# One mask tile, a gate ring of two, one scaled product on another engine and a refitted order in a fused attention and expert kernel

## The chip, the cores and the metric

The kernel runs on one core of one Trainium2 chip. The metric is the device time of one execution in microseconds; the median of three runs of the kernel before is 354.05 us (353.97 to 354.15). PE is TensorE (matrix products), ACT is ScalarE, DVE is VectorE, POOL is GpSimd and SP is SyncE. POOL and SP do little work of their own here; both mainly issue DMA transfers, each in its own fixed order.

## The reference

Four batches of eight heads, 768 tokens and 64 numbers a head go through attention with a sliding window of 128 and four sink tokens that every query sees. The result, 3072 tokens of 512 numbers, goes through four experts, each a layer 512 to 1024 with a ReLU and a layer 1024 to 512. Every expert sees every token, and its output is scaled by the token's share for it.

```python
keep = is_sink | in_window                    # 4 sinks, window of 128
scores = np.where(keep, q @ k.T / sqrt(D), -1e9)
a = softmax(scores); attn = a @ v             # per batch and head
x = attn.transpose(0, 2, 1, 3).reshape(B * S, H * D)
p = domain_probs / domain_probs.sum(-1, keepdims=True)
out = sum(p[:, e:e+1] * (np.maximum(x @ w1[e], 0) @ w2[e]) for e in range(4))
```

## The kernel before

**Work.** Each batch b has three groups g of 256 tokens. Attention of a group and a pair of heads is a scores step (L708, 64-row matmuls, `sps`), an exponential on ACT (L733, `aT`), a product with a 0/1 mask on DVE (L727, L742), a values step (L767, L774, `od`), a normalization (L801 to L819, `onat`) and a transposition into `xT`, by PE (L838) or by a DMA transpose (L791). A `sinks` step (L669) needs the transposed keys and queries `qkT` of all six token blocks of its batch. An expert's work on one group is a unit (b, g, e). The first two groups of batch 0 (the early groups) run plainly: the first layer at L1118, the second at L1579, with the outputs scaled on DVE as they are summed over the experts (L1589 for expert 0, L1591 for the others). All other groups use a form with seven products in place of eight (P1 to P7) in both layers. Their first layer either has tokens in the columns ("gated", L1208, with DVE multiplying by the token's share from a `gates` tile, L1241) or is "turned" (L1320, with the share as a scale per row on ACT or DVE, L1338, L1341, L1345, and a DMA transpose of the result). There are 20 units of each kind. The second layer of both is L1493, and the sums of its operands are formed at L1434.

**Loads.** POOL issues the loads of weights (L331, L341), of q and k (`qkn`, L251) and of v (L318). SP issues the DMA transposes of `qkn` to `qkT` (L263), the loads of `gates` (L478), the DMA transposes of turned units and the stores of `out`. A batch's transposes overwrite the `qkT` of the batch before and so wait for its last scores. Loads of `qkn` reuse buffers that the transposes free. After the last transpose of a batch, POOL makes a tiny copy (`held`, L1703), so that the next batch's loads start behind it.

**Gates.** A `gates` tile holds the shares of one unit's 256 tokens, repeated over 128 partitions, 128 KB. There are `NGATE` of them, used in turn; the load for a unit waits until the unit that used the tile before it has finished.

**Masks.** Three tiles are used: `low` (the mask in a form that PE can add to the scores, for batch 0's first group), `mask0` for group 0 and `mask1` for groups 1 and 2. The order of the blocks in `GROUPS` fixes which columns of a scores tile are which block.

**Order.** All engines run an order that is written out when the kernel is built. A planner in the kernel keeps a clock per engine (`t["pe"]`, `t["act"]`, ...), with lengths that are constants in the code, and appends PE's next step by priorities (`DUE`, `LEAD`, `SHARE_OF`, `LOW_PRODUCT`, ...). Work of ACT and DVE goes into a list with the time at which it can start and how long it may wait, and is taken out by that due time:

```python
def later(engine, ready, slack, run):
    pend.append((ready, ready + slack, engine, run))
```

So a different constant moves steps on every engine, and each engine's own waits do the rest on the chip.

Of the kernel before, what the change touches and what calls it, by code (L numbers as in the profile page):

```python
# [16 lines left out]
def kernel(  # L17
# [12 lines left out]
    nc = tc.nc  # L30
# [33 lines left out]
    EXPERTS = {(1, 0): (0, 2, 1, 3), (1, 1): (3, 2, 1, 0), (1, 2): (3, 2, 1, 0), (2, 2): (2, 0, 3, 1), (3, 1): (3, 2, 1, 0)}  # L64
# [7 lines left out]
    LOW_SECOND = 2.7  # L72
    HIGH_PRODUCT = 1.9
    EARLY = -0.01
    MASK = 5000
    GATE = 800
    GATE0 = 300
    FORM = 6000
    TOKEN = 3000
    MARGIN = 500  # L80
    HOLD = 0
    FULL = 7
    STEP0 = 0.03
    READY = 40
    REST = 3000
    LANDS = 0
    SCALED = 300
    SHARED = 2
    MARGIN1, MARGIN2 = 4000, 14000
    OWNED_READ = 152  # L90
    WIDE = 2
    OPEN = 2.5
    SOON = 34000
    NEARLY = 2
# [5 lines left out]
    ONE = 2  # L100
    HOLDS = 2
    MORE = 2
    BOTH = 1
    PAIR = 0
    OVER = 4
    ALONE = 2.0
    BEHIND = 1500
    CHORES = 3
    BIASED = 1
# [89 lines left out]

    landed = {}  # L200
    ROW = {64: 12.8, 128: 22.6, 256: 41.7, 512: 79.8, 1024: 156.2}

    def lands(key, rows, cols, *deps):
        issued = pool(0, *deps, fixed=880)
        at = max(t["sw"], issued + 1500)
# [253 lines left out]

    gate_sb = {}  # L460
    gate_tiles = [consts.tile([P, 2, 2, P], FP32, name=f"gates{i}") for i in range(NGATE // 2)]

# [8 lines left out]
    def load_gate(pair, e):  # L471

        i = len(gate_sb) % NGATE
        x = gate_tiles[i // 2][:, i % 2]
        if FIRST <= len(gate_sb) < NGATE:
            nc.vector.memset(x[0:1, 0, 0:1], 0.0)
            dve(1, fixed=150)
        nc.sync.dma_start(  # L478
            out=x.rearrange("p t n -> p (t n)"), in_=gate_rows[pair, e].rearrange("t n -> (t n)").partition_broadcast(P),
        )  # L480
        gate_sb[pair, e] = x
        sp(takes=300)

# [26 lines left out]
    for tb in (2, 3):  # L510
# [18 lines left out]
    LOW = 32768.0  # L529
    low = [lent[:, 5 * P:8 * P], lent[:, 8 * P:12 * P]]  # L530
    nc.vector.tensor_scalar(
        out=low[0].rearrange("p (n q) -> p n q", n=3)[:, 0::2], in0=two, scalar1=LOW, scalar2=-LOW, op0=ALU.mult, op1=ALU.add,
    )
    nc.vector.tensor_scalar(out=low[0][:, P:2 * P], in0=own, scalar1=-LOW, scalar2=None, op0=ALU.mult)
    nc.vector.memset(low[0][0:NSINK, 0:2 * P], 0.0)
    nc.vector.reduce_sum(
        out=sel2, in_=ident.rearrange("p (n c) -> p n c", c=32)[:, :, 0:2 * NSINK].rearrange("p n (a j) -> p n a j", a=2), axis=AX.X,
    )
    x = low[1].rearrange("p (n c q) -> p n c q", n=2, c=2)
    nc.scalar.activation(out=x[:, :, 0], in_=two, func=AF.Copy, scale=-LOW)  # L540
    nc.scalar.activation(out=x[:, :, 1], in_=two, func=AF.Copy, scale=LOW, bias=-LOW)
    mask0 = consts.tile([P, 3 * P], BF16, name="mask0")
    mask1 = consts.tile([P, 4 * P], BF16, name="mask1")
    made = []

    def make_mask(i):
        def run(engine):
            x = (mask0, mask1)[i]
            if i:
                nc.scalar.activation(out=x, in_=low[i], func=AF.Copy, scale=1 / LOW, bias=1.0)  # L550
                act(4 * P)
            else:
                nc.vector.tensor_scalar(out=x, in0=low[i], scalar1=1 / LOW, scalar2=1.0, op0=ALU.mult, op1=ALU.add)
                dve(3 * P)
            made.append(i)
        later(("dve", "act")[i], (24000.0, 11700.0)[i], 8000, run)
# [132 lines left out]
    def scores(b, hp, g, more=False):  # L689
# [10 lines left out]
        if biased:  # L700
            for ph in range(2):
                nc.tensor.matmul(sps[ph][:, 0:w], lhsT=ident, rhs=low[min(g, 1)], start=True, stop=False, skip_group_check=True)
            pe(2 * w, ready, n=2)
# [18 lines left out]
        if b == 0:  # L722
            part = join(2, masked)
        else:
            def mask_both(at):
                def run(engine):
                    nc.vector.tensor_mul(a, a, m[:, None, :].to_broadcast([P, 2, w]))  # L727
                    masked(dve(2 * w, rate=1.92))
                later("dve", at, MASK, run)
            part = join(2, mask_both)  # L730
        for ph in range(2):
            def run(engine, ph=ph):
# [8 lines left out]
                def mask_one(engine):  # L741
                    nc.vector.tensor_mul(a[:, ph], a[:, ph], m)  # L742
                    part(dve(w, rate=1.92))
# [216 lines left out]
    class Mixture:  # L960


        def __init__(self):
# [13 lines left out]
            mine = [u for u in self.order if u[0] >= OWN]  # L977
            self.turning = set(mine[TURNED_UNITS[0]:len(mine) - TURNED_UNITS[1]])
            self.gated = [u for u in self.order if u not in self.turning]
            self.G, self.resting = {}, []  # L980
            self.T, self.T_at, self.fast, self.finished = {}, {}, {}, set()
# [43 lines left out]
        def opened(self, b, g, e):  # L1025
# [11 lines left out]
            def complete(at):  # L1037
                self.H_at[b, g, e] = at
                self.finished.add((b, g, e))
                if (b, g) >= PAIRS[0]:  # L1040
                    self.waiting.append((b, g, e))
                    load_gates()
                    if not TURNED_UNITS[1] and self.gated[-1] == (b, g, e):
                        self.rest_gates()
# [39 lines left out]
        def emit_first(self, what, ready):  # L1084
# [56 lines left out]
            def run(engine):  # L1141
# [5 lines left out]
                part(at)  # L1147
            later("dve", end, GATE0, run)

# [32 lines left out]
        def emit_fast(self, u, m, ready):  # L1182
# [40 lines left out]
            def gated(dst, src, half_, ready, slack, slot=None, then=None):  # L1223
# [16 lines left out]
                def run(engine):  # L1240
# [44 lines left out]
        def emit_turning(self, u, m, ready):  # L1285
# [47 lines left out]
            def gated(k, s, src, ready, slack, slot=None, then=None):  # L1333
                gate = own_gates[:, 2 * ((b - OWN) * NG + g) + s, e:e + 1]

                def run(engine):
                    if engine == "act":
                        nc.scalar.activation(out=src, in_=src, func=AF.Relu)  # L1338

                        def scaled(engine):  # L1340
                            nc.scalar.mul(X[k][:, :, s], src, gate)  # L1341
                            done(act(n))
# [3 lines left out]
                    done(dve(n, fixed=OWNED_READ))  # L1346

                def done(at):
                    if slot is not None:
                        take(slot, at)  # L1350
# [40 lines left out]
        def chore(self):  # L1391
# [40 lines left out]
            def form(engine):  # L1432
                x = steps.pop(0)
                x[0](*x[1:])  # L1434
                at = dve(QF * P, self.stored[-1] if (b, g) == PAIRS[0] else 0.0, rate=1.92)
                if steps:
                    go(form, self.until(b, g, e, "P6 P7".split()[len(steps) == 2]))
# [128 lines left out]
        def emit_second(self):  # L1566
# [20 lines left out]
            def run(engine):  # L1587
                if e == 0:
                    nc.vector.tensor_scalar(out=dst, in0=op, scalar1=sc, scalar2=None, op0=ALU.mult)  # L1589
                else:  # L1590
                    nc.vector.scalar_tensor_tensor(  # L1591
                        out=dst, in0=op, scalar=sc, in1=dst, op0=ALU.mult, op1=ALU.add,
                    )
# [5 lines left out]
            later("dve", end, 400, run)  # L1599
            self.since = 0  # L1600
# [36 lines left out]
    work = [sum(NFB * NDB * G * (1 if (b, g) < START[e] else 7 / 8) + NFB * NDB * G * (1 if (b, g) < PAIRS[0] else 7 / 8) for g in range(NG) for e in range(E)) for b in range(B)]  # L1637
    ahead, upto, loaded, wide, rowed = 0, 0.0, 0, 0, 0
    asked = []
# [22 lines left out]
    while mix.more() or att.more():  # L1662
# [28 lines left out]
        if x and t["pool"] < now + 1500 and free_ring(x):  # L1691
            loads.remove(x)
            x[0](*x[1:])
        if turns and (ahead < 2 or not mix.second) and landed.get(("qk", *turns[0]), 1e12) < now and (turns[0][0] <= ahead or turns[0][0] == ahead + 1 and not att.todo):
# [7 lines left out]
            if 0 < b < B - 1 and x[1] == NQB - 1:  # L1702
                nc.gpsimd.tensor_copy(out=held, in_=qkT[b][:, 1, NHP - 1, S - 2:S])  # L1703
                pool(2, turned_at[x])
                nat_loads(b + 1, range(NQB))
                turns += [(b + 1, tb) for tb in range(NQB)]
        flush(now)
        mix.tokens()
# [3 lines left out]
        if ahead + 1 < B and not att.more() and (ahead == 0 or (ahead + 1, 0) in turned_at) and (ahead == 0 or mix.done >= sum(work[:ahead]) * LEAD[ahead - 1]):  # L1712
            ahead += 1
            if ahead == 1:
                own_load()
            elif ahead == 2:
                own_made()
            att = Attention(ahead)
# [79 lines left out]
```

## Time and profile before

| | |
|---|---|
| median of three runs | 354.05 us |
| span of the profiled execution, first to last instruction | 351.9 us |
| outside the span (the median less the span) | 2.15 us |
| PE busy, share of the span | 346.2 us, 98% |
| DVE busy | 282.8 us, 80% |
| ACT busy | 208.3 us, 59% |
| POOL busy | 71.6 us, 20% |
| granted TensorE clock | 1.000 |
| moved by DMA | 45.61 MB, mean 130 GB/s |

A time of the profiled execution itself is not given beside its span; the median of the runs stands for it, and the 2.15 us between the two are taken as fixed. Busy time is the union of an engine's instructions. Matmuls overlap one another and their ends are modelled, so a busy PE can still have small pauses in it; they show only in the distances between the starts. In a row of the groups, the first part names the line, the engine, the operation and the tiles, then come the count, the busy time, the mean length of one in ns, and the idle time just before them with what ended it.

### The profile page before, as it was taken

To read this page: it belongs to the slowest core of one execution; us is meant where nothing else is said; L and a number is where in the kernel's file an instruction comes from. 1 tells how busy PE (TensorE), PEld (TensorE's weight loads), DVE (VectorE), ACT (ScalarE), POOL (GpSimd) and SP (SyncE) were. 2 spreads that over 40 slices of the span, in tenths; PEclk is the share of its full clock that TensorE was granted. 3 is DMA by queue.
4 is the path that set the end of the run, shared out by engine and by line. 5 is a ranking of instruction groups with operands and counts; after the bars stand their busy time and mean duration, and the time that the engine had idled before them with its cause. 6 is when DMAs were issued, how large, how long until landed. Compare 5 with 4: busy or idle time off the path is not lost.

```text
span 351.9 us, 9351 instructions
## 1 busy us (share of the span) xinstructions
PE 346.2 (98%) x3721; PEld 266.0 (76%) x3721; DVE 282.8 (80%) x672; ACT 208.3 (59%) x476; POOL 71.6 (20%) x89
## 2 busy tenths in 40 slices
PE   8999999999999999999999999999999999999996
PEld 3685769656789998998999886755856676666685
DVE  5886999878999999799898999578768586675740
ACT  6863624447874443647453539689589767666611
POOL 8946114330546206100152000000000000000000
PEclk9999999999999999999999999999999999999999
DMA  9999999999999999920999602545437733545441
GB/s 178 178 188 195 223 214 181 179 160 174 162 147 165 121 145 122 132 64 9 109 173 159 113 32 62 120 101 120 80 91 174 127 89 93 120 120 115 67 120 61
DMA packets 161032, 45.61 MB, mean 130 GB/s; under 512 B 144740, under 2 KB 156996, under 8 KB 160988
## 3 DMA queue, kind: packets, MB, share of 16 engines
q0 software_dynamic: 79104, 17.31, 56.4%
q1 hardware_dynamic: 80828, 27.18, 40.1%
q8 instruction: 29, 0.48, 0.5%
q10 hardware_dynamic: 1056, 0.52, 0.5%
q14 instruction: 15, 0.12, 0.1%
HBM read 38.39 MB, written 6.34 MB: 127 GB/s over the span
## 4 chain that ended last, share of the span: by engine, by line
PE 75%; DMA 19%; POOL 5%; issue 1%; ACT 0%; POOLq 0%; SPq 0%
PE acc L1493 35%; PE cps L1320 17%; PE cps L1208 15%; DMA w<-in_moe_w_dram 12%; DMA qkn<-in_k_dram 4%; DMA qkT<-qkn 3%; PE sps L708 3%; PE od L774 2%; POOL qkn L251 2%; POOL w L331 1%; POOL vx L318 1%; PE hps L1118 1%; PE od L767 1%; POOL w L341 0%; PE acc L1579 0%
## 5 line engine op out<-in xcount | busy, mean ns | idle before, releaser
L1493 PEld LDWEIGHTS <-H 128*128 128x128 bf16 x708 | 66.5, 98 | 17.9 <-issue 1.1
L1493 PE MATMUL acc<-w,H 128*128 128x256 bf16 x420 | 56.9, 273 | 0.0
L733 ACT ACTIVATE aT<-sps 128x512 bf16<-128x512 f32 (+1 forms) x96 | 47.2, 579 | 16.3 <-PE sps L708 16.2
L1208 PEld LDWEIGHTS <-w 128*128 128x128 bf16 x640 | 39.1, 98 | 1.2 <-issue 0.5
L1493 PEld LDWEIGHTS <-S 128*128 128x128 bf16 x320 | 30.3, 98 | 9.5 <-issue 0.8
L1241 DVE SCALAR_TENSOR_TENSOR H<-cps,gates 128x512 bf16<-128x512 f32 x54 | 36.6, 683 | 0.0
L1338 ACT ACTIVATE cps<-cps 128x512 f32<-128x512 f32 x44 | 25.5, 585 | 17.5 <-PE cps L1320 17.0
L1118 PE MATMUL hps<-xT,w 128*128 128x256 bf16 x256 | 31.9, 273 | 0.1
L819 ACT ACTIVATE onat<-od,R 128x64 bf16<-128x64 f32 x108 | 24.9, 324 | 11.4 <-DVE R L801 11.1
L318 POOL DMA_DIRECT2D vx<-in_v_dram x24 | 21.4, 903 | 43.0 <-PE od L774 31.2
L1208 PEld LDWEIGHTS <-vf 128*128 128x128 bf16 x480 | 29.3, 98 | 1.0 <-issue 0.5
L1579 PE MATMUL acc<-w,H 128*128 128x512 bf16 x128 | 29.9, 379 | 0.0
L1493 PE MATMUL acc<-wf,H 128*128 128x256 bf16 (+1 forms) x216 | 29.6, 272 | 0.0
L1118 PEld LDWEIGHTS <-w 128*128 128x128 bf16 x256 | 24.1, 98 | 4.7 <-issue 0.9
L1341 ACT ACTIVATE rest<-cps,own_gates 128x512 bf16<-128x512 f32 x37 | 25.5, 693 | 0.7
L727 DVE TENSOR_TENSOR aT<-aT,mask 128x1024 bf16<-128x1024 bf16 (+1 forms) x36 | 22.7, 640 | 3.1 <-ACT aT L733 2.8
L251 POOL DMA_DIRECT2D qkn<-in_q_dram x22 | 19.7, 896 | 23.3 <-DMA qkT<-qkn 14.7
L1208 PE MATMUL cps<-T,w 128*128 128x128 bf16 x320 | 24.3, 219 | 0.0
L1208 PE MATMUL cps<-xT,w 128*128 128x128 bf16 x320 | 24.1, 219 | 0.0
L1320 PE MATMUL cps<-w,T 128*128 128x512 bf16 x80 | 23.8, 379 | 0.0
L1320 PE MATMUL cps<-vf,T 128*128 128x512 bf16 x80 | 23.6, 379 | 0.0
L1554 ACT COPY osb<-acc 128x256 f32<-128x256 f32 x32 | 12.1, 382 | 19.3 <-PE acc L1493 19.1
(145 smaller groups left out, 673.5 us busy)
## 6 DMA issues: line engine op xcount, KB each, us to landing
w<-in_moe_w_dram POOLq DMA_DIRECT2D x6, 1024.0 KB, 18.4
out_dram<-osb SPq DMA_DIRECT2D x16, 256.0 KB
vx<-in_v_dram POOLq DMA_DIRECT2D x24, 128.0 KB, 6.5
qkn<-in_q_dram POOLq DMA_DIRECT2D x22, 128.0 KB, 6.7
qkn<-in_k_dram POOLq DMA_DIRECT2D x22, 128.0 KB, 7.4
gates<-gate_rows SPq DMA_DIRECT2D x20, 128.0 KB
w<-in_moe_w_dram POOLq DMA_DIRECT2D x4, 256.0 KB, 6.9
w<-in_moe_w_dram POOLq DMA_DIRECT2D x2, 512.0 KB, 11.5
```

Of the source, the lines that this page charges most:

```text
L251: nc.gpsimd.dma_start(out=both[:, i], in_=src[b, :, tb * P:(tb + 1) * P, :].rearrange("h p d -> p h d"),)
L318: nc.gpsimd.dma_start(out=vx[tb][:, :, 0:D], in_=v[b, :, tb * P:(tb + 1) * P, :].rearrange("h p d -> p h d"),)
L733: nc.scalar.activation(out=a[:, ph], in_=sps[ph][:, 0:w], func=AF.Exp, scale=scale)
L819: nc.scalar.mul(o[:, qi, hp, ph * D:(ph + 1) * D], od[:, qi, ph, 0:D], R[:, qi, ph])
L1118: nc.tensor.matmul(h[:, i].rearrange("p (q n) -> p q n", q=2), lhsT=w1_sb[e][:, db, fb * P:(fb + 1) * P], rhs=xT[b, g][:, :, db], start=(i ...
L1208: nc.tensor.matmul(y[:, f], lhsT=A[:, d, f * P:(f + 1) * P], rhs=T[:, d], start=(m in ("P1", "P5") and f == 0 and d == 0), stop=(d == 1), ...
L1241: nc.vector.scalar_tensor_tensor(out=dst, in0=src, scalar=0.0, in1=gate, op0=ALU.max, op1=ALU.mult)
L1320: nc.tensor.matmul(y.rearrange("p f n -> p (f n)"), lhsT=T[:, d], rhs=A[:, d], start=(m in ("P1", "P5") and d == 0), stop=(d == 1), skip_g ...
L1338: nc.scalar.activation(out=src, in_=src, func=AF.Relu)
L1341: nc.scalar.mul(X[k][:, :, s], src, gate)
L1493: nc.tensor.matmul(y, lhsT=self.operand(b, g, e, m)[:, f], rhs=forms[e][m][:, f, cs], start=(k == 0 and f == 0 and m in (("P1", "P5", "P2" ...
L1579: nc.tensor.matmul(op, lhsT=H[:, fb // QF, fb % QF, s], rhs=w2_sb[e][:, fb, :], start=(fb == 0), stop=(fb == NFB - 1),)
```

## The change

`GROUPS[0]` lists its two entries the other way round, so that both masks are views of one tile `masks`, and products with it repeat it over several blocks. The `gates` ring goes from four tiles to two, and the DMA memory set aside for rows of turned units becomes two tiles of their own plus one gates tile. The scaled product of expert 0 in the early groups goes from DVE to ACT. `own_gates` is loaded for one batch more and finished a fixed time after its load. A `hold()` before q, k and v loads is added, but with `HELD = 9` no batch reaches it. The planner gets longer lengths for ACT and DVE, a landing time for gates, and new constants, which move steps on all engines. The kinds and counts of PE's matmuls stay the same but for one idle filler.

```diff
     GROUPS = [
-        [(0, 0, 2), (1, 1, 1)],
+        [(1, 1, 1), (0, 0, 2)],
...
-    NGATE = 4
+    NGATE = 2
-    OWN = 2
-    TURNED_UNITS = (4, 0)
+    OWN = 1
+    TURNED_UNITS = (0, ... 16 times, 1, ... 20 times)
+    EXPERTS = {...}   # another order of experts in eleven groups
-    MIX = 6
-    SHARE_OF = (1.01, 0.92, 0.96)
-    LEAD = (1.01, 0.99)
-    DUE = 1.9
+    MIX = 9
+    SHARE_OF = (1.08, 0.92, 0.94)
+    LEAD = (0.96, 1.035)
+    DUE = 1.5
...
-    MASK = 5000
-    GATE = 800
-    GATE0 = 300
-    FORM = 6000
-    TOKEN = 3000
-    MARGIN = 500
+    MASK = 10000
+    GATE = 1300
+    GATE0 = 1500
+    FORM = 12500
+    TOKEN = 5250
+    MARGIN = 100
...
-    OWNED_READ = 152
+    OWNED_READ = 218
+    OWNS = 26000
+    HALVES = 2
+    HELD = 9
+    GATE_LANDS = 600
...
     def act(cols, *deps):
-        t["act"] = at + max(196, 68 + cols / 1.23)
-        return at + max(350, 205 + cols / 1.2)
+        t["act"] = at + max(200, 76 + cols / 1.23)
+        return at + max(375, 230 + cols / 1.2)
     def dve(cols, *deps, rate=0.96, fixed=157):
-        t["dve"] = at + fixed - 85 + cols / rate
-        return at + fixed + 35 + cols / rate
+        t["dve"] = at + fixed - 77 + cols / rate
+        return at + fixed + 60 + cols / rate
...
-        sp(takes=300)
+        gate_at[pair, e] = sp(takes=300) + GATE_LANDS
...
-    x = low[1].rearrange("p (n c q) -> p n c q", n=2, c=2)
-    nc.scalar.activation(out=x[:, :, 0], in_=two, func=AF.Copy, scale=-LOW)
-    nc.scalar.activation(out=x[:, :, 1], in_=two, func=AF.Copy, scale=LOW, bias=-LOW)
-    mask0 = consts.tile([P, 3 * P], BF16, name="mask0")
-    mask1 = consts.tile([P, 4 * P], BF16, name="mask1")
+    masks = consts.tile([P, 4 * P], BF16, name="masks")
+    mask0, mask1 = masks[:, P:], masks[:, 0:2 * P]
...
-                    nc.vector.tensor_mul(a, a, m[:, None, :].to_broadcast([P, 2, w]))
+                    x = a if g == 0 else a.rearrange("p h (r c) -> p (h r) c", r=2)
+                    nc.vector.tensor_mul(x, x, m[:, None, :].to_broadcast([P, 2 if g == 0 else 4, w if g == 0 else 2 * P]))
...
-                later("dve", ready, slack, run)
+                later("dve", max(ready, gate_at[b * NG + g, e]), slack, run)
...
                 if e == 0:
-                    nc.vector.tensor_scalar(out=dst, in0=op, scalar1=sc, scalar2=None, op0=ALU.mult)
+                    nc.scalar.mul(dst, op, sc)
+                    acc_free[bank] = act(Dout)
+                    return
```

More of the change, by code (lines that the diff above doesn't have):

```diff
@@ L58 @@
     ]
-    NGATE = 4
+    NGATE = 2
     TURN_ABOUT = 1
-    OWN = 2
-    TURNED_UNITS = (4, 0)
-    EXPERTS = {(1, 0): (0, 2, 1, 3), (1, 1): (3, 2, 1, 0), (1, 2): (3, 2, 1, 0), (2, 2): (2, 0, 3, 1), (3, 1): (3, 2, 1, 0)}
+    OWN = 1
+    TURNED_UNITS = (0, 0, 0, 0, 0, 0, 0, 0, 0, 0, 0, 0, 0, 0, 0, 0, 1, 1, 1, 1, 1, 1, 1, 1, 1, 1, 1, 1, 1, 1, 1, 1, 1, 1, 1, 1)
+    EXPERTS = {(1, 0): (0, 2, 3, 1), (1, 1): (0, 2, 1, 3), (1, 2): (1, 3, 0, 2), (2, 2): (0, 2, 3, 1), (3, 1): (0, 2, 1, 3), (3, 2): (3, 0, 1, 2), (2, 0): (1, 0, 3, 2), (0, 2): (0, 1, 3, 2), (3, 0): (2, 3, 1, 0), (2, 1): (0, 2, 3, 1), (0, 1): (2, 1, 0, 3)}
     FIRST = 1
     START = {0: (1, 0), 1: (0, 2), 2: (0, 0), 3: (1, 0)}
-    MIX = 6
-    SHARE_OF = (1.01, 0.92, 0.96)
-    LEAD = (1.01, 0.99)
-    DUE = 1.9
+    MIX = 9
+    SHARE_OF = (1.08, 0.92, 0.94)
+    LEAD = (0.96, 1.035)
+    DUE = 1.5
     LOW_PRODUCT = 2.9
-    LOW_SECOND = 2.7
-    HIGH_PRODUCT = 1.9
-    EARLY = -0.01
-    MASK = 5000
-    GATE = 800
-    GATE0 = 300
-    FORM = 6000
-    TOKEN = 3000
-    MARGIN = 500
+    LOW_SECOND = 3.2
+    HIGH_PRODUCT = 1.4
+    EARLY = -0.05
+    MASK = 10000
[4 more added lines that the diff above has]
+    MARGIN = 100
     HOLD = 0
-    FULL = 7
-    STEP0 = 0.03
+    FULL = 8
+    STEP0 = 0.3
     READY = 40
-    REST = 3000
-    LANDS = 0
-    SCALED = 300
+    REST = 4000
+    LANDS = -1400
+    SCALED = 100
     SHARED = 2
     MARGIN1, MARGIN2 = 4000, 14000
-    OWNED_READ = 152
+    OWNED_READ = 218
[3 more added lines that the diff above has]
+    GATE_LANDS = 600
     WIDE = 2
-    OPEN = 2.5
-    SOON = 34000
+    OPEN = 1.7
+    SOON = 23000
     NEARLY = 2
@@ L100 @@
     ONE = 2
-    HOLDS = 2
+    HOLDS = 1
     MORE = 2
@@ L104 @@
     PAIR = 0
[L105 to L108, printed above, removed]
+    OVER = 7
+    ALONE = 1.6
+    BEHIND = 2300
+    CHORES = 2
     BIASED = 1
@@ L200, with marked, hold @@
     landed = {}
+    mark = []
+    def marked(at, x):
+        mark[:] = [at, x]
+    def hold():
+        nc.gpsimd.tensor_copy(out=held, in_=mark[1])
+        pool(2, mark[0])
     ROW = {64: 12.8, 128: 22.6, 256: 41.7, 512: 79.8, 1024: 156.2}
@@ L204, in lands @@
         issued = pool(0, *deps, fixed=880)
-        at = max(t["sw"], issued + 1500)
+        at = max(t["sw"], issued + 800)
         t["sw"] = at + rows * ROW[cols] / 16
@@ L529 @@
     LOW = 32768.0
-    low = [lent[:, 5 * P:8 * P], lent[:, 8 * P:12 * P]]
+    low = lent[:, 5 * P:8 * P]
     nc.vector.tensor_scalar(
-        out=low[0].rearrange("p (n q) -> p n q", n=3)[:, 0::2], in0=two, scalar1=LOW, scalar2=-LOW, op0=ALU.mult, op1=ALU.add,
+        out=low.rearrange("p (n q) -> p n q", n=3)[:, 0:2], in0=two, scalar1=LOW, scalar2=-LOW, op0=ALU.mult, op1=ALU.add,
     )
-    nc.vector.tensor_scalar(out=low[0][:, P:2 * P], in0=own, scalar1=-LOW, scalar2=None, op0=ALU.mult)
-    nc.vector.memset(low[0][0:NSINK, 0:2 * P], 0.0)
+    nc.vector.tensor_scalar(out=low[:, 2 * P:], in0=own, scalar1=-LOW, scalar2=None, op0=ALU.mult)
+    nc.vector.memset(low[0:NSINK, P:], 0.0)
     nc.vector.reduce_sum(
@@ L547, in run @@
         def run(engine):
-            x = (mask0, mask1)[i]
             if i:
-                nc.scalar.activation(out=x, in_=low[i], func=AF.Copy, scale=1 / LOW, bias=1.0)
-                act(4 * P)
-            else:
-                nc.vector.tensor_scalar(out=x, in0=low[i], scalar1=1 / LOW, scalar2=1.0, op0=ALU.mult, op1=ALU.add)
-                dve(3 * P)
+                nc.scalar.activation(out=masks[:, 0:P], in_=own, func=AF.Copy, scale=-1.0, bias=1.0)
+                nc.scalar.copy(out=masks[:, P:2 * P], in_=own)
+                act(P)
+                act(P)
+            else:
+                nc.vector.tensor_scalar(out=masks[:, 2 * P:], in0=low[:, P:], scalar1=1 / LOW, scalar2=1.0, op0=ALU.mult, op1=ALU.add)
+                dve(2 * P)
             made.append(i)
@@ L701, in scores @@
             for ph in range(2):
-                nc.tensor.matmul(sps[ph][:, 0:w], lhsT=ident, rhs=low[min(g, 1)], start=True, stop=False, skip_group_check=True)
+                nc.tensor.matmul(sps[ph][:, 0:w], lhsT=ident, rhs=low, start=True, stop=False, skip_group_check=True)
             pe(2 * w, ready, n=2)
@@ L726, in run @@
                 def run(engine):
-                    nc.vector.tensor_mul(a, a, m[:, None, :].to_broadcast([P, 2, w]))
-                    masked(dve(2 * w, rate=1.92))
+                    x = a if g == 0 else a.rearrange("p h (r c) -> p (h r) c", r=2)
+                    nc.vector.tensor_mul(x, x, m[:, None, :].to_broadcast([P, 2 if g == 0 else 4, w if g == 0 else 2 * P]))
+                    at = dve(2 * w, rate=1.92)
+                    marked(at, a[:, 1, w - 2:w])
+                    masked(at)
                 later("dve", at, MASK, run)
@@ L977, in __init__ @@
             mine = [u for u in self.order if u[0] >= OWN]
-            self.turning = set(mine[TURNED_UNITS[0]:len(mine) - TURNED_UNITS[1]])
+            self.turning = {u for u, x in zip(mine, TURNED_UNITS) if x}
             self.gated = [u for u in self.order if u not in self.turning]
-            self.G, self.resting = {}, []
+            self.G = {}
+            self.resting = [(0.0, mo.tile([P, QF, 2, P], BF16, name=f"row{i}", tag=f"row{i}", bufs=1)) for i in range(HALVES)]
             self.T, self.T_at, self.fast, self.finished = {}, {}, {}, set()
@@ L1042, in complete @@
                     load_gates()
-                    if not TURNED_UNITS[1] and self.gated[-1] == (b, g, e):
+                    if self.gated[-1] == (b, g, e):
                         self.rest_gates()
@@ L1147, in run @@
                 part(at)
-            later("dve", end, GATE0, run)
+            later("dve", max(end, gate_at[b * NG + g, e]), GATE0, run)
         def tokens(self):
@@ L1341, in scaled @@
                             nc.scalar.mul(X[k][:, :, s], src, gate)
-                            done(act(n))
+                            done(act(n + 125))
                         later("act", act(n), SCALED, scaled)
@@ L1345, in run @@
                     nc.vector.tensor_scalar(out=X[k][:, :, s], in0=src, scalar1=0.0, scalar2=gate, op0=ALU.max, op1=ALU.mult)
-                    done(dve(n, fixed=OWNED_READ))
+                    done(dve(n, fixed=OWNED_READ) if slot is not None else dve(n, rate=1.92, fixed=214))
                 def done(at):
+                    marked(at, X[k][:, 0, s, 0:2])
                     if slot is not None:
@@ L1588, in run @@
                 if e == 0:
[L1589 to L1593, printed above, removed]
+                    nc.scalar.mul(dst, op, sc)
+                    acc_free[bank] = act(Dout)
+                    return
+                nc.vector.scalar_tensor_tensor(
+                    out=dst, in0=op, scalar=sc, in1=dst, op0=ALU.mult, op1=ALU.add,
+                )
                 acc_free[bank] = at = dve(Dout, fixed=218)
@@ L1598, in run @@
                     self.stored.append(sp(at))
-            later("dve", end, 400, run)
+            later("dve" if e else "act", end, 400, run)
             self.since = 0
@@ L1637 @@
     work = [sum(NFB * NDB * G * (1 if (b, g) < START[e] else 7 / 8) + NFB * NDB * G * (1 if (b, g) < PAIRS[0] else 7 / 8) for g in range(NG) for e in range(E)) for b in range(B)]
-    ahead, upto, loaded, wide, rowed = 0, 0.0, 0, 0, 0
+    ahead, upto, loaded, wide, rowed, owned = 0, 0.0, 0, 0, 0, 1e12
     asked = []
@@ L1692 @@
             loads.remove(x)
+            if x[0] is not load_w1 and x[0] is not load_w2 and x[1] >= HELD:
+                hold()
             x[0](*x[1:])
@@ L1706 @@
                 turns += [(b + 1, tb) for tb in range(NQB)]
+        if owned + OWNS < now:
+            owned = 1e12
+            own_made()
         flush(now)
@@ L1715 @@
                 own_load()
-            elif ahead == 2:
-                own_made()
+                owned = now
             att = Attention(ahead)
```

6 lines of the change are left out of this document (4 added, 2 removed).

## The prediction

> **What bounds the kernel now.** I read the page's shares and slices, then the chain that ended last, then the groups by form, then the timelines of PE, POOL and SP where the chain leaves PE. First the page: busy time, the 40 slices, the shares of the chain.
>
> ```profile
> PE 346.2 (98%) x3721; PEld 266.0 (76%) x3721; DVE 282.8 (80%) x672; ACT 208.3 (59%) x476; POOL 71.6 (20%) x89
> PE   8999999999999999999999999999999999999996
> DVE  5886999878999999799898999578768586675740
> PEclk9999999999999999999999999999999999999999
> DMA  9999999999999999920999602545437733545441
> PE 75%; DMA 19%; POOL 5%; issue 1%; ACT 0%; POOLq 0%; SPq 0%
> ```
>
> TensorE is the bound: nine tenths or more in nearly every slice, at a clock of 1.0. VectorE is nearly full in slices 7 to 15 (about 58 to 130 us), and the DMA engines are full up to about 66 us and again around 80 to 105 us. The chain's pieces in order of time say where a DMA set PE's date:
>
> ```profile
> 12.30 12.54 DMA w<-in_moe_w_dram
> 28.52 28.81 DMA w<-in_moe_w_dram
> 57.60 2.60 POOL qkn L251 x3
> 60.20 14.86 DMA qkn<-in_k_dram
> 75.11 10.75 DMA qkT<-qkn
> ```
>
> These 69 us do not mean that PE stood still for 69 us. PE was busy at the same time and stopped only at the last link. PE's timeline at that place, with the idle time in brackets:
>
> ```profile
> 85.99 0.29 PE L669 MATMUL sinks<-qkT,ksd 128*32 128x256 bf16 x4 [0.30 <-DMA qkT<-qkn]
> ```
>
> Counting the distance from each matmul's start to the next, less its columns at the steady rate (256 columns in 109 ns, as in the chain's "103.44 2.62 PE acc L1493 x24"), I find 9.7 us in which PE did not stream. Some 6 us are entries to and exits from the 64-row score steps (64 of them, 95 ns each); about 1.4 us are the first 4 us, where matmuls of 128x512 take longer; 1.7 us are short stops before 16 us. After that only some 1.4 us are stops for data: 0.25 at 20.3, 0.22 at 21.9, 0.14 at 79.2, 0.37 at 85.3, 0.12 at 102.3, 0.08 at 140, 0.27 at 240.8 to 242.4. So no change of order or of another engine's load can bring much over 1.5 us, unless it shortens the start or the 3.4 us behind the last matmul's start, and both stay as they are; what it can lose has no such limit.
>
> **The change, part by part.** The span is 351.9 us and the median of the runs 354.05, so 2.15 us lie outside the span; I sum on the span and add them back.
>
> *PE's own work.* In the written-out order PE has one 128x256 idle filler more (+0.11 us at 109 ns) and enters or leaves score steps 66 times instead of 64 (2 x 95 ns = +0.19). Everything else is equal in count and shape: **+0.30 us**, on the path in full.
>
> *One mask tile.* Two ScalarE preparations, the old second mask and part of the first go (416 + 399 + 632 ns on ScalarE), two 128x128 copies come (under 324 ns each, the row of the 128x64 normalizations). All of it lies before the masks are first used, ScalarE is at 59%, and the activation table's load still starts first: 0. The 52 mask products keep their sizes and now read a mask repeated in pieces of 256.
>
> ```profile
> L727 DVE TENSOR_TENSOR aT<-aT,mask 128x1024 bf16<-128x1024 bf16 x24 | 16.3, 686 | 3.0 <-ACT aT L733 2.8
> L1434 DVE TENSOR_TENSOR H<-H 128x512 bf16<-128x512 bf16 x35 | 14.7, 420 | 0.0
> L1589 DVE TENSOR_SCALAR osbw<-acc,scale_t 128x512 f32<-128x512 f32 x4 | 3.0, 746 | 2.7 <-PE acc L1579 2.7
> L1338 ACT ACTIVATE cps<-cps 128x512 f32<-128x512 f32 x44 | 25.5, 585 | 17.5 <-PE cps L1320 17.0
> L1341 ACT ACTIVATE rest<-cps,own_gates 128x512 bf16<-128x512 f32 x37 | 25.5, 693 | 0.7
> ```
>
> The L1434 sums read strided pieces of 128 and run at 420 ns for 512 columns, the same rate as the masks, so I take 0. If the repeated operand halved the rate, 24 x 0.65 + 12 x 0.49 + 16 x 0.33 us (746 ns of f32 against 420 for 512 columns is 0.33 per 512) would put some 27 us on VectorE, most of it before 180 us, where it is full; that is the upper bound, and as no row points to it, it gets no chance of its own.
>
> *First scaled product to ScalarE.* Four times 746 ns leave VectorE (3.0 us), four times 585 to 693 ns come to ScalarE (2.3 to 2.8 us). ScalarE's slices there are 4 to 8 tenths, so they fit. PE waits for neither beyond the stops above: 0, and 3.0 us of cover for VectorE where it is scarcest.
>
> *Gates, loads and rows.* The two early gate loads of 128 KB less lighten the queues before 40 us; own_gates grows from 12 to 18 columns of 4. Expert 3's second weights landed at 69.2 us before and are first needed at PE work 63.9 instead of 69.1, about 69.6 us: just in time, 0 to +0.5. Turned units get two row tiles of their own beside one gate tile, three halves in place of two, so the distance from a transpose to its use grows (smallest 5.2 to 7.0 us of PE work): 0.
>
> *The refitted order.* Adding up the matmuls before each step, the sinks step that waited 0.37 us at 85.3 moves 2.5 us later (79.6 to 82.1), with the same transposes ahead of it; the pairs behind the stops at 79, 102, 140 and 241 us, where ScalarE or VectorE had 0.10 to 0.13 us of PE work, now have 0.2 or more. I take these five, 0.37 + 0.14 + 0.12 + 0.08 + 0.27 = **-0.95 us** (bounds: all seven with the start's, -1.7; none, 0). The start changes only in places: a filler in place of a 0.12 stop, one transposition group later by 0.2: 0, within 0.3 either way.
>
> *Gate ring of two.* Twenty gate loads as before, but load k+2 now waits for the last gating of unit k. Where VectorE had 20 us or more of work between that release and the first use, it has 5 to 14 from the fourth on (smallest 5.2, 6.6, 7.0). SP issues in order, so a load also waits behind what stands before it:
>
> ```profile
> 100.83 4.47 SPq L263 DMA_TRANSPOSE qkT<-qkn  x2
> 121.57 12.03 SPq L263 DMA_TRANSPOSE qkT<-qkn  x2
> 133.70 2.20 SPq L478 DMA_DIRECT2D gates<-gate_rows  x3
> ```
>
> Before, three gate loads stood 12 us behind a transpose that waited for its load, and nobody noticed. In the new order the tightest is the load behind batch 2's first two transposes. Those wait for batch 1's last scores, at PE work 107.2 (about 113.5 us, against 94.0 and 100.5 before); they hold SP 4.5 us, so the gates are issued at about 118.0. PE needs the gated H at work 115.0, 121.4 us, so the gates must be there by 120.7. The trace has no landing time for a gate load. Below, it lands in time, 0; above, it takes the 7.4 us of the 128 KB k loads in the software queue, lands at 125.4 and costs 4.7. Nearest is the transpose on the same queue, issued at 131.67 and landed at 134.9, 3.2 us: 121.2, a stop of 0.5 to 0.6. The gates' longer rows are fewer packets, so I take half, **+0.30**. [...]
>
> Sum: +0.30 - 0.95 + 0.30 = -0.35. Span 351.55, time **353.7**.
>
> **The rivals.**
>
> *Batch 2's q/k chain comes late (slower).* Its six transposes hang on that same release, 13 us later than before, while the sinks step that needs all six moves only from 139.5 to about 142 us. POOL shows the chain before:
>
> ```profile
> 108.38 0.88 POOL L251 DMA_DIRECT2D qkn<-in_q_dram  x1 [6.56 <-DMA qkT<-qkn]
> 114.44 0.94 POOL L251 DMA_DIRECT2D qkn<-in_q_dram  x1
> 135.00 0.18 POOL L1703 COPY held<-qkT 128x2 bf16<-128x2 bf16 x1 [18.75 <-DMA qkT<-qkn]
> ```
>
> From the first transpose's issue (100.83) to the last one landed (135.00) it took 34.2 us; the new window is 142 - 113.5 = 28.5. Past 28.5 us each us stops PE: at 34.2, +5.7, 359.4. For it: the same loads, and the same stores on SP between them. Against: of the 34.2 us, 7.5 went by before the first load was issued and 16 between the last one's issue (115.3) and its landing (131.6), with vx loads queued ahead of or between the q/k loads; now those are done or stand behind. I expect 22 to 28 us. [...] Chance 0.15, likeliest price 2 to 3 us, about 356.
>
> *The gate ring (slower).* The gate load above takes over 3.5 us, or several of the tight ones do; VectorE stands in order, with the masks and additions that PE needs queued behind the gating. It decides from 120.7 us on: +1 to +4 beyond the sum, likeliest 355.2. For: a margin under 1 us, twenty loads. Against: VectorE is 3 us lighter, 16 of 19 margins exceed 7.5 us. Chance 0.17.
>
> *The stops of the start go too (faster).* Half of the 1.7 us before 16 us and the 0.47 at 20 to 22: -1.0 more, 352.7. Against: the loads and engines there are unchanged. Chance 0.08.
>
> That the change doesn't do what it says is excluded for counts, since the order shows them; that all stops only move elsewhere is the upper end of the forecast, +0.6, 354.3.
>
> **How the numbers follow.** The forecast has 0.60, with a range of its own of 353.0 to 354.5. What a measurement here can tell from no change is 0.2%, 0.7 us: under 353.34 is faster, over 354.76 slower. Faster: 0.26 of the forecast's 0.60 and 0.07 of the early rival, 0.33. Slower: 0.05 + 0.14 + 0.15 = 0.34. Same: 0.33. The range 352.6 to 356.5 leaves out about 0.04 below and 0.14 above.
>
> **What would show it.** Right: PE's busy sum up 0.3, no wait of sinks for qkT at 85, stops behind 16 us of 0.5 us in all, VectorE's scaled products down to none. Wrong: a wait of VectorE's gating for a gates DMA, at 120 us above all; a wait of PE for qkT at 142; mask products over 700 ns; PE waiting for w at 69.

## The result and the profile after

The changed kernel takes 358.56 us (median of four runs, 356.65 to 362.84) against 354.09 for the kernel before. The ratio is 1.0111 with a 95% interval of 1.0080 to 1.0142. It is slower, and it spreads: before, all runs lie within 0.2 us. The ratios, here and below, are of fast runs alone, without executions over 1.5% above the fastest of their kernel, such as the one of 362.84 us. The profiled execution was the longest of the four, 362.84 us with a span of 361.1, so 1.7 us lie outside the span. The same difference holds in all later profiles, where the prediction took 2.15.

The page of the changed kernel, the lines that answer to those of before:

```profile
PE 350.2 (97%) x3722; PEld 269.1 (75%) x3722; DVE 285.3 (79%) x676; ACT 201.7 (56%) x458; POOL 72.2 (20%) x89
PE   8999999999999996999997999999999999999996
PEclk9999999999999998999999899999999999999999
DMA  9999999999979999970399903509628944646431
PE 85%; DMA 6%; DVE 5%; SPq 1%; issue 1%; ACT 1%; POOL 0%; POOLq 0%; DVEq 0%; ACTq 0%
```

Two slices of PE have a hole (135 to 144 us and 190 to 199). The granted clock falls in the first of them and in the slice behind the second (199 to 208). VectorE, which was nowhere in the chain, now has 5% of it. Its waits name the reason (in all, times, longest):

```profile
DVE H L1256 <- DMA gates<-gate_rows: 4.9, 3, 2.9
```

Before, there was no such wait. The lengths of the mask products and of the moved scaled product are as forecast (the groups by form):

```profile
L738 DVE TENSOR_TENSOR aT<-aT,masks 128x1024 bf16<-128x1024 bf16 x24 | 16.1, 683 | 0.6 <-ACT aT L746 0.5
L1606 ACT ACTIVATE osbw<-acc,scale_t 128x512 f32<-128x512 f32 x4 | 2.8, 688 | 4.2 <-PE acc L1596 4.2
```

### The profile page after: what moved, and what is told of

It is laid out like the page before. It is cut to its first block, busy times and chain, and to the rows that moved or that the text cites. A ratio compares the mean times of both kernels' runs of the same rounds, so it can differ in the third digit from the quotient of the medians.

```text
span 361.1 us, 9320 instructions
## 1 busy us (share of the span) xinstructions
PE 350.2 (97%) x3722; PEld 269.1 (75%) x3722; DVE 285.3 (79%) x676; ACT 201.7 (56%) x458; POOL 72.2 (20%) x89
## 3 DMA queue, kind: packets, MB, share of 16 engines
q0 software_dynamic: 79104, 17.31, 54.4%
q1 hardware_dynamic: 81596, 27.19, 43.4%
## 4 chain that ended last, share of the span: by engine, by line
PE 85%; DMA 6%; DVE 5%; SPq 1%; issue 1%; ACT 1%; POOL 0%; POOLq 0%; DVEq 0%; ACTq 0%
PE acc L1510 32%; PE cps L1335 17%; PE cps L1223 14%; PE acc L1596 8%; PE hps L1133 7%; DMA gates<-gate_rows 5%; PE sps L718 3%; PE od L788 2%; DMA vx<-in_v_dram 2%; DVE H L1256 1%; SPq L275 1%; PE od L781 1%; DVE aT L756 1%; PE tx L852 1%; DVE H L1291 1%
## 5 line engine op out<-in xcount | busy, mean ns | idle before, releaser
L1510 PEld LDWEIGHTS <-H 128*128 128x128 bf16 x732 | 69.8, 99 | 19.4 <-issue 1.7
L1510 PE MATMUL acc<-w,H 128*128 128x256 bf16 x432 | 58.9, 275 | 0.0
L1510 PEld LDWEIGHTS <-S 128*128 128x128 bf16 x320 | 31.1, 99 | 9.4 <-issue 0.2
L833 ACT ACTIVATE onat<-od,R 128x64 bf16<-128x64 f32 x100 | 23.1, 325 | 19.6 <-DVE R L815 19.6
L1353 ACT ACTIVATE cps<-cps 128x512 f32<-128x512 f32 x39 | 22.6, 586 | 15.3 <-PE cps L1335 15.1
L1223 PE MATMUL cps<-T,vf 128*128 128x128 bf16 x320 | 23.1, 219 | 2.3 <-DVE H L1256 2.3
L1335 PE MATMUL cps<-w,xT 128*128 128x512 bf16 x80 | 23.8, 379 | 0.0
L738 DVE TENSOR_TENSOR aT<-aT,masks 128x1024 bf16<-128x1024 bf16 (+1 forms) x36 | 22.5, 639 | 1.4 <-ACT aT L746 1.2
```

The costliest lines, as they stand in the source:

```text
L738: nc.vector.tensor_mul(x, x, m[:, None, :].to_broadcast([P, 2 if g == 0 else 4, w if g == 0 else 2 * P]))
L833: nc.scalar.mul(o[:, qi, hp, ph * D:(ph + 1) * D], od[:, qi, ph, 0:D], R[:, qi, ph])
L1223: nc.tensor.matmul(y[:, f], lhsT=A[:, d, f * P:(f + 1) * P], rhs=T[:, d], start=(m in ("P1", "P5") and f == 0 and d == 0), stop=(d == 1), ...
L1335: nc.tensor.matmul(y.rearrange("p f n -> p (f n)"), lhsT=T[:, d], rhs=A[:, d], start=(m in ("P1", "P5") and d == 0), stop=(d == 1), skip_g ...
L1510: nc.tensor.matmul(y, lhsT=self.operand(b, g, e, m)[:, f], rhs=forms[e][m][:, f, cs], start=(k == 0 and f == 0 and m in (("P1", "P5", "P2" ...
```

## The experiments

### The changed kernel again, four tiles, an earlier place, held loads

Three edits of the changed kernel were run with it. The first gives the gates four tiles (the second pair shares memory with a row tile) and leaves every engine's order as it is. The second also issues each load where a ring of four would, and leaves all but SyncE's order.

```diff
# e1: four tiles (the line that picks the tile)
-        i = len(gate_sb) % NGATE
+        i = (len(gate_sb) + 2) % 4
# e2: four tiles, and the load is issued two units earlier (the condition of its issue)
+            len(issued) < (4 if t["pe"] > GATED else FIRST) or mix.gated[len(issued) - 4] in mix.finished
# e3: loads held
-    HELD = 9
+    HELD = 2
```

The unaltered kernel, e0:

> The changed kernel once more, unaltered, to see how its runs spread. Theory A (the gate ring): VectorE's gating waits for gates DMAs near 135 to 140 us and near 194 us, PE stops 2 to 3 us behind each, and the spread of the runs (356.65 to 358.95 us so far) comes from how long these loads take to land, 7 to 9 us. Theory B (the q/k chain of batch 2): the stop at 140 us is seen by sinks waiting for qkT instead. Theory C (the refitted order loses by itself): the loss is spread over many small stops. Time 356.5 to 359.

e1, four tiles, same place:

> Four gates tiles in place of two, with every engine's order exactly as in the changed kernel, SyncE's queue too: a gate load keeps its place in the queue, it only no longer waits for the last gating of the unit two before it. Theory A in the form 'the wait for the tile': the two stops of 2 to 3 us go, 353.5 to 354.5. Theory A in the form 'the place in the queue and the landing': the load at about 130 us still stands behind the same transposes and lands 7 to 9 us later, so the stops shrink by at most 1 us each, 355 to 357.5. Theories B and C: no change, 356.5 to 359.

e2, four tiles, two units earlier:

> Four gates tiles, and each gate load moved two units earlier in SyncE's queue, as a ring of four would have it; all other engines keep the changed kernel's order (VectorE has two one-element memsets more). Theory A: no wait of VectorE for gates is left, both stops go, 353.0 to 354.2. Theory B: the sinks step of batch 2, which needs all six transposes, now waits for qkT at about 142 us by 1 to 3 us, 355 to 356.5. Theory C: 355.5 or more with stops at many places.

e3, loads held:

> The changed kernel with HELD = 2: every load of q, k and v for batches 2 and 3 stands on GpSimd behind a tiny copy from VectorE's newest result, so the loads no longer come as one bunch of nine behind the first transpose (119 to 127 us). The planner shifts a few steps from about 60% of the order on. Theory A with slow landing because of that bunch: the gate loads land in under 5 us, the stops shrink, 354 to 356. Theory A with the release alone: no change, 356.5 to 359. Theory B: the chain of batch 2 gets later, 358 or more.

Measured: e0 358.77 us (ratio 1.0131, 1.0086 to 1.0176), e1 358.61 (1.0130, 1.0103 to 1.0157), e2 **353.90 (1.0005, 0.9996 to 1.0014)**, e3 358.91 (1.0140, 1.0125 to 1.0155). e1 came out above the 355 to 357.5 that I gave to the place in the queue, and e3 above the 354 to 356 of held loads.

In e0's timelines of VectorE and of PE, the brackets give the wait ahead of an instruction:

```profile
121.87 0.69 DVE L1256 SCALAR_TENSOR_TENSOR H<-cps,gates 128x512 bf16<-128x512 f32 x1 [0.64 <-DMA gates<-gate_rows]
138.99 0.69 DVE L1256 SCALAR_TENSOR_TENSOR H<-cps,gates 128x512 bf16<-128x512 f32 x1 [1.46 <-DMA gates<-gate_rows]
191.87 0.69 DVE L1256 SCALAR_TENSOR_TENSOR H<-H,gates 128x512 bf16<-128x512 f32 x1 [2.70 <-DMA gates<-gate_rows]
```

```profile
139.74 0.34 PE L718 MATMUL sps<-qkT 64*128 64x128 bf16 x3 [1.23 <-DVE H L1256]
193.21 1.05 PE L1223 MATMUL cps<-T,vf 128*128 128x128 bf16 x16 [2.13 <-DVE H L1256]
```

Each late gate load holds VectorE, and PE stands behind it: by the distances of the matmuls' starts 0.53 us at 122.0, 1.39 at 138.3 and 2.30 at 190.8. SyncE's timeline and e0's chain say why the second is late:

```profile
126.05 1.20 SPq L1499 DMA_DIRECT2D out_dram<-osb  x1
127.34 0.44 SPq L490 DMA_DIRECT2D gates<-gate_rows  x1
127.89 1.93 SPq L275 DMA_TRANSPOSE qkT<-qkn  x1
130.26 0.33 SPq L490 DMA_DIRECT2D gates<-gate_rows  x1
130.69 8.01 SPq L275 DMA_TRANSPOSE qkT<-qkn  x2
```

```profile
130.26 8.71 DMA gates<-gate_rows
184.66 7.12 DMA gates<-gate_rows
```

The load is issued at 130.26 and lands 8.71 us later. The one of 184.66 takes 7.12, and it was issued at the very moment when VectorE's last gating of the unit two before it ended (184.64). In e1 that tile wait is gone, and the same two loads read:

```profile
129.48 9.08 DMA gates<-gate_rows
183.81 6.09 DMA gates<-gate_rows
```

They are issued less than 1 us earlier, because the transposes and stores ahead of them in SyncE's queue set the time, and they still take 6 to 9 us. The median of e1 is that of e0 within 0.2 us, so the tile wait alone is not the loss. (The two profiles differ by more, since e1's is of its second shortest run and e0's of one above its median.) The place in SyncE's queue, two units too near to the use for such a landing, is: e2 moves only the place on top of e1, and nothing waits for gates any more. The whole loss is gone, 4.9 us of the median. PE's windows (busy time, count, and as the third last number the granted clock) show the second stop in e0 and the same steps in e2:

```profile
190.00:195.00 5.00, 2.87 (x39) 2.49 (x37) 3.13 (x8) 1.12 (x5) 2.63 (x3) 0.95 1.86 156
195.00:200.00 5.00, 5.00 (x44) 4.04 (x43) 3.89 (x9) 0.72 (x3) 0.00 (x0) 0.71 1.71 193
```

```profile
187.00:192.00 5.00, 5.00 (x72) 4.72 (x71) 4.99 (x12) 2.13 (x7) 2.93 (x4) 1.00 1.55 176
192.00:197.00 5.00, 5.00 (x60) 4.61 (x58) 5.00 (x13) 0.74 (x2) 0.00 (x0) 1.00 2.49 167
```

In e0 the stop has a tail. From 194.55 to 197.96 us matmuls of 256 columns start 213 ns apart in place of 109, which costs 1.67 us more. With it the spans add up, from e2's 352.2: e0 has 0.53 + 1.39 + 2.30 of stops and 1.67 of half rate, 358.1 (358.2 measured). e1 has 1.67 + 0.81 + 0.26 and no half rate, 354.9 (355.0). The profile on record has 0.64 + 2.75 + 2.47 and 3.2 in two stretches of half rate, 361.3 (361.1). By these three profiles, the spread of the runs is how late these loads land and whether the clock falls after it.

e3 tells nothing about the landing: the copies that should hold the loads found VectorE's results already there, and the nine loads of batch 2 went out between 120.5 and 129 us, as before. The stops stayed (0.51, 1.18, 2.52).

### Why the gates land late

POOL's loads go through a queue of their own, the software queue (q0, `software_dynamic`, 79104 packets and 17.31 MB in e0); those of q, k and v move in packets of 128 bytes (69632 of the 79104 in the profile on record). SyncE's go through a hardware queue (q1, `hardware_dynamic`, 81596 packets and 27.19 MB in e0), here called its ring. e4 fetches the same bytes of q and k in rows of 1 KB; e8 also leaves out v for batches 2 and 3. e9 moves the gate loads to another queue, and e10 tells the planner of 7 us.

```diff
# e4: q and k of batches 2 and 3
-                out=both[:, i], in_=src[b, :, tb * P:(tb + 1) * P, :].rearrange("h p d -> p h d"),
+                out=both[:, i].rearrange("p h d -> p (h d)"), in_=rows.rearrange("(p n) -> p n", p=P),
# e8: e4, and
+            if b < 2:
                 nc.gpsimd.dma_start(out=vx[tb][:, :, 0:D], ...)
# e9: load_gate
-        nc.sync.dma_start(
+        nc.scalar.dma_start(
# e10
-    GATE_LANDS = 600
+    GATE_LANDS = 7000
```

> The changed kernel with a ring of two, in which the q and k loads of batches 2 and 3 fetch the same bytes as 128 rows of 512 numbers instead of 1024 rows of 64 (so batches 2 and 3 attend over differently placed numbers; all instructions, orders and waits stay). Theory 'the landing is slow because SyncE's ring gets only a small share while 1024 short packets of each such load wait in the software queue': the gates land within 4 us of their issue, the stops at 138 and 190 us fall under 1 us in all, 353.5 to 355. Rival 'the gates are slow because of the stores and transposes ahead of them in SyncE's own ring': landing stays 7 us or more, 356.5 to 359.

> As the run with q and k in rows of 512 numbers, and the v loads of batches 2 and 3 are left out too (these batches use batch 1's v), so that no short packets stand in the software queue behind 115 us. In the run before, the stop at 190 us had gone and one of 1.2 us at 139 us stayed, with three v loads of 1024 short packets beside it. Theory 'the short packets of the software queue make the gates late': the gates at 131 us land within 5 us, the stop at 139 goes too, 353.6 to 355. Rival 'what stands ahead in SyncE's own ring (a store, transposes) is enough': the stop of 1 us or more stays, 355 to 356.5.

> The changed kernel, ring of two, with the 20 gate loads issued by ScalarE in place of SyncE, at the same places of the written order: they no longer stand behind SyncE's transposes and stores, but still share the DMA engines with the software queue, and ScalarE now waits for the tile. Theory 'SyncE's queue and ring ahead of the gates make half of the delay': gates land in 3 to 5 us, 354 to 356. Rival 'sharing with the software queue alone does it': landing stays 7 us, 356 to 359. Rival 'ScalarE stands waiting for VectorE's gating, and PE with it': 357 or more, with waits of ScalarE for VectorE.

> The changed kernel, ring of two, with GATE_LANDS = 7000 in place of 600: the planner takes a gate load to land 7.3 us after its issue, and places VectorE's gatings after that. Theory A with 'the place and the landing': the planner now puts other work in between, stops for gates fall, 354 to 356.5. Rival 'a ring of two has no room for 7 us whatever the order': the stops move into PE's written order, as idle PE without a named gate wait or as gate waits again, 356 to 360.

Measured: e4 356.11 us (1.0068, 1.0044 to 1.0092), e8 355.10 (1.0036, 1.0025 to 1.0047). e4 lies between the ranges of its theory and its rival. e8's median lies 0.1 us inside the rival's, while its profile, of its shortest run (354.14 us), is as the theory has it; where the other 1 us of its usual runs goes was not seen. In e4 the stop at 190 us is gone; 1.21 at 139 us stays, where v loads in 128-byte packets still stand beside the gates, and the stop at 122 us is longer than in e0, 1.41 against 0.53. In e8's profile only 0.51 at 121.7 stays. That is the load behind the first two transposes of batch 2. In e0 it landed in 3.36 us, with no software packet beside it; in e4 it has 87 of 1 KB beside it, in e8 65. Its lines in the chains of e4 and e8:

```profile
118.39 4.30 DMA gates<-gate_rows
117.77 3.75 DMA gates<-gate_rows
```

So long rows are no cure for every load. But at 139 and 190 us the short packets of the software queue make the difference, and the packets of e0 alone say the same. Six of its gate loads behind 110 us have no software packets beside them (issued at 118.48, 154.74, 157.47, 165.69, 169.76 and 201.46); their last data came 2.6 to 3.0 us after the issue. Four have some 3500 to 4000 beside them (127.34, 130.26, 184.66 and 185.85), and their last data came after 5.5 to 8.0 us. In the profile on record it is 2.5 to 3.2 us for the six without any (117.68, 157.50, 160.23, 168.46, 172.53 and 204.39) and 5.5 to 8.2 us for the four beside some 3000 to 4100 (126.76, 130.81, 187.42 and 188.61).

In e0's packets from 186 to 188 us, the software queue moved 1567 packets of 128 bytes and SyncE's ring 119 of 2 KB, the store that stands ahead of the gates; the gates' first packet came after 188. In e4, in the same 2 us, the counts are 231 (of 1 KB) and 167. The sums are 13 to 1 and 1.4 to 1, and the ratio does not hold within them: in e0 the first of the two us has 374 short packets to 118 long ones, the second 1193 to 1. How the two queues share the DMA engines was not shown.

e9 took 369.47 us, and its time settles nothing about the landing. ScalarE, in order, stood 9.8 us behind an early gate load whose rows were not yet written, and PE behind ScalarE. But a later load in e9's chain does bear on it (waits first, then the chain):

```profile
PE hps L1133 <- ACT H L1146: 9.0, 1, 9.0
```

```profile
142.57 9.81 DMA gates<-gate_rows
```

On ScalarE's queue no store and no transpose of SyncE stands ahead of this load, and it still takes 9.81 us, with 3609 short packets of the software queue and SyncE's transposes beside it. So what stands ahead in SyncE's ring is not needed for a slow landing.

e10 took 358.03 us (1.0119, 1.0102 to 1.0136). Its waits have no gates left, but others:

```profile
PE cps L1223 <- DVE cps L1276: 0.8, 1, 0.8
PEld L1335 <- DVE H L1256: 0.8, 1, 0.8
```

With two tiles and 7 us the planner finds no order that keeps PE busy. The stops moved into the order (0.94 at 128.7, 0.57 at 150.2, 1.4 in four near 158, 0.64 at 211.5).

### What the other parts are worth

On top of e2, e5 puts the two ScalarE preparations back and e6 the scaled product on VectorE. e7 gives the planner itself the ring of four, and e11 is the kernel before once more.

```diff
# e5
+    nc.scalar.activation(out=x[:, :, 0], in_=two, func=AF.Copy, scale=-LOW)
+    nc.scalar.activation(out=x[:, :, 1], in_=two, func=AF.Copy, scale=LOW, bias=-LOW)
# e6
-                    nc.scalar.mul(dst, op, sc)
+                    nc.vector.tensor_scalar(out=dst, in0=op, scalar1=sc, scalar2=None, op0=ALU.mult)
# e7
-    NGATE = 2
+    NGATE = 4
```

> The version with four tiles and earlier gate loads, and the two ScalarE preparations that the mask part took out (two 128x256 operations before the first k cast) put back, writing where nothing reads. In all runs without them the first k cast starts at 5.05 to 5.25 us, with them, before, at 4.70. Theory 'taking them out made the start 0.4 us longer': the cast starts at about 4.7 us and the time falls by 0.3 to 0.6 us, to 353.3 to 353.6. Rival 'the start differs for another reason, such as the transposition group that was moved': 353.8 to 354.0.

> The version with four tiles and earlier gate loads, with the four first scaled products of the early groups back on VectorE at the same places of the order. Theory 'they cost PE nothing on either engine': 353.7 to 354.1. Rival 'VectorE is short of time before 130 us and the 3.0 us matter': 354.3 to 355.5. Rival 'ScalarE was the worse place': under 353.6.

> The changed kernel with NGATE = 4, so that the planner itself knows the ring of four and refits its order (second row tile and second gates tile share memory). Theory A: no wait for gates, 353.2 to 354.5, as the version with the earlier loads or a little better. Rival 'the refit finds worse places elsewhere': 354.5 to 357 with stops that are not at gates.

> The kernel before, unaltered, for a profile beside these runs. In its first profile the first k cast on ScalarE starts at 4.70 us, in all profiles of the changed orders at 5.05 to 5.25. If that is the change, the cast starts at 4.70 again; if it is the transfer's own spread, at 4.7 to 5.2. Time 353.4 to 354.2.

Measured: e5 353.91 us (1.0004, 0.9995 to 1.0013), e6 353.89 (1.0004, 0.9995 to 1.0014), e7 353.80 (0.9999, 0.9991 to 1.0008), e11 353.73. None of them differs from before by more than can be told. With a ring of four, the new order, the mask tile and the product's place are together worth nothing that shows. The first k cast on ScalarE, in e11 and in e2:

```profile
4.82 0.62 ACT L287 CAST qkn<-kraw 128x512 bf16<-128x512 f32 x1 [0.26 <-DMA kraw<-in_k_dram]
```

```profile
5.08 0.62 ACT L299 CAST qkn<-kraw 128x512 bf16<-128x512 f32 x1 [1.85 <-DMA kraw<-in_k_dram]
```

In e5, with the preparations back, it starts at 5.17, so they are not the reason. The profiles of the changed order have 5.00 to 5.25, the two of before 4.70 and 4.82. Why this transfer lands some 0.2 to 0.5 us later stays open.

## Why the prediction was wrong

**The forecast's gate term failed.** It was +0.30 us and measured +4.9 (e0 against e2). It went wrong in three places.

- The landing. I took 3.2 us from a transpose issued at 131.67. At that moment the last q and k load had just landed (131.62), so the software queue was empty (in the kernel before it has no packet from 131.6 to 135.0 us). The gates that matter are issued while loads of q, k and v are queued (nine of them go out from 119.2 to 129.1 us in e0), and take 6 to 9 us. The upper bound of 7.4 us was in the text, but was used for one load only.
- Which loads. I priced the one behind batch 2's first transposes, and there the price was right: 0.5 to 0.6 us forecast, 0.53 in e0 and 0.51 in e8. I gave the other tight ones (the smallest margin was 5.2 us) no term, and counted margins over 7.5 us as safe. In e0 VectorE was ready to use the load of 130.26 when the tile had been free for 7.3 us, and the load took 8.71; for the first of the pair at 184.66 the two are 4.5 and 7.12.
- The price of a stop. I counted an idle microsecond as one. Stops of 2.30 us in e0 and of 2.75 and 2.47 in the profile on record were followed by stretches at half clock, 1.6 to 1.7 us lost in each.

**The ring rival** had the mechanism (a late gate, VectorE in order, PE behind it) with a chance of 0.17 and a time of 355.2; it came out 3.4 us worse, for the same three reasons.

**The refitted order** was forecast at -0.95 with PE's own work at +0.30. The stops that I named did go, but there was less of them, and others came. My five terms add up to 0.98 (I wrote 0.95, and the parts that I named of the 9.7 us add up to 10.5); counted in the same way they are 0.63 in e11, because the one at 85 us was 0.03 there and 0.37 only in the first profile. In e2 three new ones stand behind 24 us: 0.18 at 36, 0.15 at 179 and 0.14 at 211 us. The start, which I took as 0, came 0.34 us later (the stop of the first products at 22.48 in e2, 22.14 in e11). So +0.30 - 0.63 + 0.47 + 0.34 = +0.48, and the spans of the two profiles differ by 0.43 (352.19 against 351.76). By the medians it is +0.05 (353.90 against 353.85), as e11's profile is of its shortest run. The order's gain was 0.16 us in place of 0.95, and the start took it back.

**Batch 2's chain** was judged rightly, if narrowly. In e2 its first transpose is issued at 114.23, and the last has landed before these two lines (POOL, then PE):

```profile
140.14 1.31 POOL L1735 COPY held<-qkT 128x2 bf16<-128x2 bf16 x1 [11.96 <-DMA qkT<-qkn]
```

```profile
142.49 0.40 PE L691 MATMUL sinks<-qkT,ksd 128*32 128x512 bf16 x4
```

That is 25.9 us where I expected 22 to 28, with 2.3 us to spare. **The masks** (683 against 686 ns) cost PE nothing, as said. **The scaled product** (688 ns) was not quite free: the stop of 0.18 us at 36 us is PE waiting for an exponential that ScalarE runs behind the last of the four products, and neither the kernel before nor e6 has it. It is too small for the medians (e2 353.90, e6 353.89).

## What to carry to other kernels

A ring's depth is the distance from release to use, and it must cover the slowest landing in the busiest stretch, not that of a free queue (in e0 5.5 to 8.0 us against 2.6 to 3.0): look for the load's landing where other queues hold many short packets, and for what stands ahead of it in its own queue. Price every member of the ring against that, not the tightest alone. When more buffers do not help, check whether the load is also issued earlier; here four tiles in the old place were worth nothing (358.61 us against 358.77) and the earlier place everything (353.90).

## What was not expected of the hardware

- The same 128 KB gate load has its last data 2.6 to 3.0 us after its issue with no software packets beside it, and 5.5 to 8.0 us after it beside some 3500 to 4000 packets of 128 bytes (e0). By the chains, the loads that stopped VectorE beside such packets landed in 6.1 to 9.4 us (e1, the profile on record), and in 9.8 us from ScalarE's queue (e9).
- A PE stop of 2.30 us (e0), and of 2.75 and 2.47 us (the profile on record), was followed, 0.9 to 1.5 us after PE had started again, by 3.4 us at half rate, 1.6 to 1.7 us lost; a stop of 2.52 us (e3) was not (its granted clock is 1.00 from 190 to 205 us). So the length alone does not decide. In the profile on record the changes of the granted clock between its first and its last lie 136.53, 3.41, 51.20, 3.41 and 160.43 us apart, and PE stood 1.97 and 2.47 us within the 3.41 us ahead of the two falls; in e0 it stood about 2.1 us. What decides whether the clock falls was not shown.
